# A new first stage for fused gated attention and SwiGLU: gate scratch in a tile of its own, queries and keys of batch 0 split at token 256, values cast by the transfer, weights in thirds

## The chip, the core and the metric

One core of one Trainium2 chip. The metric is device microseconds (us) of one execution of the program; lower is better.

## What is computed

```python
scores = q @ k.T / sqrt(D)                    # B, H, S, D = 8, 8, 576, 64, float32
cum    = cumsum(log(clip(f, 1e-4, 1)))        # one forget gate per token and head
scores = where(j > i, -1e9, scores + cum[i] - cum[j])
attn   = softmax(scores)
x      = (attn @ v) -> tokens x (heads*D)     # 4608 x 512
out    = (silu(x @ w_gate) * (x @ w_val)) @ w_out   # 512 -> 1536 -> 512
```

## The kernel before, in words

**The work.** Attention runs head by head, in pairs of heads (`p`, four pairs a batch). `score` (L481) multiplies 128-row blocks of keys by queries into PSUM, in four groups of blocks per head (`BANKS`). Group 0 needs only the first 256 queries and keys; groups 1 to 3 hold the rest of the triangle. Queries and keys lie transposed in the tile `QK` with 64 rows of data and four extra rows, in which the cumulated gates stand split into bf16 parts, so that the product adds the decay by itself: a score needs both the data rows and the four gate rows. `expo` (L489, ACT) takes exponentials, `mask` (L498, POOL) zeroes what lies above the diagonal, `weigh` (L512, PE) multiplies by the values in the tile `VB`, `invert` and `scale` (L519, L528, DVE) divide, and `flip` (L536, PE) and `put` write the result transposed to `xT`. The feed-forward part runs in tiles of tokens: `gate` (L613) twice per block of 128 of the 1536 columns (12 blocks, `fc`), `tanh` (ACT, L617), `silu` and `times` (DVE, L621, L624) into buffers `hh`, and `project` (L628). Batch 0's tokens are two tiles, 256 and 320 tokens, taken together block by block (`ffn(0..)`, `ffn(1..)`); after these come tiles of 512.

**The first stage.** `f` is loaded on ACT's queue (L296) into a piece of the big tile `xT`. DVE clips (L326), ACT takes logarithms (L328), DVE sums (L329) and splits the sum into parts (L331, L334, L336, L337; ACT L332). Four row transfers on ACT's queue (`row`, L341) carry the four parts for batches 0 and 1, all 576 tokens, into `QK`; `dec_out` (L351, SP) sends the parts of the other batches to memory. Queries and keys of batches 0 and 1 are loaded on SP's queue a pair of heads at a time (`ld_qk`, L364) into pieces of `xT` or of the still empty weight tile `wo`, cast to bf16 (L284), turned on PE (`turn`, L374) and copied into `QK` (`straighten`). Values are loaded in float32 on SP's queue (`ld_v`, L400) and cast by POOL, DVE or ACT. The weights `wg`, `wv`, `wo` come in quarters on POOL's queue, cast by the transfer (`weights`, L606, L609). While PE has nothing to do, up to plan time 22, it gets multiplications of no use (`dummy`, L719).

**What sets the order.** The whole order is made at build time: a small list scheduler (`Plan`) simulates the engines and queues with booked costs, gives each engine the ready operation of lowest `key`, honours `ready` times (`W_AT`, `WO_AT`, `Q1_AT`, `V1_AT`, and `release`, which admits the pairs of batches 2 to 7 at `PACE0 + n*PACE`), and hands out buffers. What it writes is one fixed instruction list per engine; on the chip each engine goes through its list in order and stops at what is not ready. Transfers of each kind (SP and ACT together, POOL alone) signal on eight semaphores in turn, so the ninth transfer waits for the first to land; the planner counts this for SP and ACT, not for POOL.

From batch 2 on, queries and keys go through memory in bf16 (`narrow`, L382, POOL's queue) and come back by transposing transfers on SP's queue (L391), with the gate rows from memory (L394).

Of the kernel before, what the change touches and what calls it, by code (L numbers as in the profile page):

```python
# [32 lines left out]
class Plan:  # L33
# [9 lines left out]
    def op(self, eng, fn, after=(), take=(), use=(), key=0.0, ready=0.0, dma=None):  # L43
        o = Op(eng, fn, list(after), list(take), list(use), key, ready, dma)
        for b in o.use:
            b.left += 1
        self.ops.append(o)
        return o
# [17 lines left out]
    def run(self, idle=None):  # L66
# [21 lines left out]
        while left:  # L88
# [4 lines left out]
            while events and events[0][0] <= t + 1e-9:  # L93
                _, _, kind, o = heapq.heappop(events)
                if kind in ("queue", "dma"):
                    busy_rings = [r for r in rings.values() if r]
                    for r in busy_rings:
                        r[0][0] -= (t - moved) / len(busy_rings)
                        while r and r[0][0] < 1e-6:
                            over, n = r.pop(0)  # L100
                            if r:
                                r[0][0] += over
                            n.done = t + 1.0
                            push(n.done, "end", n)
                            push(n.done, "done", (n, None, False))
# [4 lines left out]
                    if busy_rings:  # L110
                        push(t + min(r[0][0] for r in busy_rings) * len(busy_rings), "dma", None)
# [63 lines left out]
HALF = 256  # L175
# [11 lines left out]
PACE, PACE0 = 8.8, 70.0  # L187
# [3 lines left out]
def kernel(ctx, tc, q, k, v, f, w_gate, w_val, w_out, out):  # L191
# [16 lines left out]
    NCH = 4  # L208
# [22 lines left out]
    BF = [sb(f"BF{i}", [P, QT, 2, D], BF16) for i in range(4)]  # L231
# [3 lines left out]
    HH = [sb(f"hh{i}", [P, S], BF16) for i in range(NHH)]  # L235
# [6 lines left out]
    def ps(b):  # L242
        return bank[bank_of[b.pool] + b.i]

    early = [xT[:BH, r, S : 3 * S].bitcast(F32) for r in range(KD)]
    lf, zero, cum, r1 = early
    dec = xT[:BH, :, 3 * S : 5 * S].rearrange("p r (w s) -> p r w s", w=2)
    nat = {"nat": [xT[:QP, r, N_TOK - 2 * QT * D * 2 :].bitcast(F32).rearrange("p (h x) -> p h x", h=2) for r in range(KD)],
           "natw": [wo[:QP, KF // 4 * r : KF // 4 * (r + 1)].rearrange("p a b -> p (a b)").bitcast(F32)
                    .rearrange("p (h x) -> p h x", h=2) for r in range(4)]}  # L250
# [3 lines left out]
        {"f": 4, "s": 2, "o": 1, "t": 1, "qk": NQK, "pt0": NPT0, "pt": NPT, "vb": NVB, "nv": NNV, "nat": KD, "natw": 4, "bf": 4,  # L254
# [13 lines left out]
    def act(n):  # L268
        return 0.06 + n / 1200 + 0.06
# [31 lines left out]
    o_bf = [op(("DVE", 0.3), lambda e, i: nc.vector.memset(BF[i][QP:], 0.0), i, key=-8) for i in range(4)]  # L301

    def blank(e, what):
# [12 lines left out]
        else:  # L316
# [3 lines left out]
    o_dec = [op(("DVE", 0.3), blank, "dec", key=-7), op(("DVE", 0.9), blank, "dec1", key=-7)]  # L320
    o_qkz = op(("POOL", 0.8), blank, "qk", key=15)
    o_vb = [op(("POOL", 0.8), blank, i, key=20 + 2000 * i) for i in range(NVB)]
    o_pt = op(("POOL", 2.5), blank, "pt", key=40)
    o_edge = op(("SP", SPi), blank, "edge", after=[o_qkz], key=900, dma=0.2, ready=20)

    o_clip = op(("DVE", dve(S, False)), lambda e: nc.vector.tensor_scalar(  # L326
        out=lf, in0=lf, scalar1=1e-4, scalar2=1.0, op0=ALU.max, op1=ALU.min), after=[o_f], key=-9)
    o_ln = op(("ACT", 0.6), lambda e: nc.scalar.activation(lf, lf, AF.Ln), after=[o_clip], key=-9)  # L328
    o_scan = op(("DVE", 1.4), lambda e: nc.vector.tensor_tensor_scan(  # L329
        out=cum, data0=lf, data1=zero, initial=0.0, op0=ALU.add, op1=ALU.add), after=[o_ln, o_zero], key=-9)  # L330
    o_hi = op(("DVE", 0.7), lambda e: nc.vector.tensor_scalar_mul(dec[:, 1, 1], cum, -8.0), after=[o_scan], key=-9)  # L331
    o_up = op(("ACT", 0.6), lambda e: nc.scalar.activation(dec[:, 0, 0], cum, AF.Copy, scale=8.0),  # L332
              after=[o_scan], key=-9)
    o_r1 = op(("DVE", 0.7), lambda e: nc.vector.scalar_tensor_tensor(  # L334
        out=r1, in0=cum, scalar=-8.0, in1=dec[:, 1, 1], op0=ALU.mult, op1=ALU.subtract), after=[o_hi], key=-9)
    o_mid = op(("DVE", 0.4), lambda e: nc.vector.tensor_copy(dec[:, 2, 1], r1), after=[o_r1], key=-9)  # L336
    o_lo = op(("DVE", 0.7), lambda e: nc.vector.tensor_sub(dec[:, 3, 1], r1, dec[:, 2, 1]), after=[o_mid], key=-9)  # L337
    o_warm = op(("ACT", 1.4), lambda e: nc.scalar.activation(warm, cum[:1, :1], AF.Exp), after=[o_up], key=-9)

    def row(e, r):  # L340
        nc.scalar.dma_start(  # L341
            out=QK[D + r : D + r + 1, : FIRST * FB, :, :S].rearrange("o b (j w) s -> o (b j) w s", w=2),
            in_=dec[: FIRST * H, r].rearrange("h w s -> h (w s)"),
        )

    o_row = []
    for r, a in ((0, [o_up, o_dec[0]]), (1, [o_hi, o_dec[1]]), (2, [o_mid, o_dec[1]]), (3, [o_lo, o_dec[1]])):
        o_row.append(op(("ACT", 0.5), row, r, after=a, key=-9, dma=0.15))
# [6 lines left out]
    o_decd = op(("SP", SPi), dec_out, after=[o_up, o_lo, o_dec[0], o_dec[1]], key=60, dma=2.0)  # L355

# [6 lines left out]
    def ld_qk(e, p, nm, b):  # L363
        nc.sync.dma_start(out=nat[b.pool][b.i], in_=srcs[nm][2 * p : 2 * p + 2].rearrange("h (p t) d -> p h (t d)", t=QT))  # L364

    def cast_qk(e, bn, bb):
        dst, src = BF[bb.i][:QP].rearrange("p t h d -> p h t d"), nat[bn.pool][bn.i].rearrange("p h (t d) -> p h t d", d=D)
        copy(e, dst, src)

    def turn(e, bb, bt):  # L370
        src = BF[bb.i].rearrange("p t h d -> p t (h d)")
        t = ps(bt).bitcast(BF16)
        for n in range(QT):
            nc.tensor.transpose(t[:, n * QP : n * QP + P], src[:, n], ident)  # L374

    def straighten(e, p, x, a, bt):
        dst = QK[:D, hqk[p].i, 2 * a + x, :S].rearrange("p (c n) -> p c n", n=QT)
        src = ps(bt).bitcast(BF16)[a * D : (a + 1) * D, :S].rearrange("p (n c) -> p c n", n=QT)
        copy(e, dst, src)
# [28 lines left out]

    def values(b, n, key, after=(), ready=0.0):
        bv = Buf("nv")  # L410
        o = op(("SP", SPi), ld_v, b, n, bv, take=[bv], key=key, dma=1.53 if n < NB - 1 else 0.77, after=after,
               ready=ready)
        eng = copier(H * D, False) if b < 2 else ("POOL", pool(H * D))
# [11 lines left out]

    def queries(p, key, after=(), ready=0.0):
        done = []
        b = p // FB
        if b < FIRST:
            rest = []  # L430
            for x, nm in enumerate("qk"):
                bn, bb, bt = Buf("natw" if p in (2, 3) else "nat"), Buf("bf"), Buf("t", ("f", 30.0), ("s", 22.0))
                kk = key + 2 * x
                o1 = op(("SP", SPi), ld_qk, p, nm, bn, take=[bn], key=kk, dma=0.96, after=after, ready=ready + 0.9 * x,
                        tag=("ldqk", p))
                o2 = op({"POOL": 0.85, "DVE": 0.87} if p else ({"POOL": 0.85} if x else {"DVE": 0.87}), cast_qk, bn, bb,
                        after=[o1] + o_bf, take=[bb], use=[bn], key=kk, tag=("cast", p))
                if p in (2, 3):
                    wo_free.append(o2)
                o3 = op(("PE", mm(*[P] * QT)), turn, bb, bt, after=[o2, o_id], take=[bt], use=[bb], key=kk,  # L440
                        tag=("turn", p))
                for a in range(2):
                    first = not rest and not a
                    rest.append(op(
                        {"ACT": 0.65, "DVE": 0.75}, straighten, p, x, a, bt,
# [20 lines left out]
        else:  # L466
            done = done + o_row
        for j in range(2):
            q_ready[2 * p + j] = done
# [75 lines left out]
    def attention(p, key, parts):  # L545
# [3 lines left out]
        for n, (bks, qb, nq) in enumerate(parts):  # L549
# [5 lines left out]
            for j in range(2):  # L555
# [4 lines left out]
                for m, i in enumerate(bks):  # L560
# [5 lines left out]
                    a = op(("PE", mm(*cols)), score, h, i, bs, after=q_ready[h] + ([o_qkz] if i == 2 else []), take=[bs], use=[hqk[p]],  # L566
# [5 lines left out]
                    a = op(("POOL", 0.33), mask, h, i, after=[a], use=[hp], key=kk, tag=("mask", h, i))  # L572
# [26 lines left out]
            x_ready[p, qb] = op({"DVE": dve(m)} if not ahead else copier(m), put, p, bt, qb, nq, after=[a, ] + early_done,  # L599
# [23 lines left out]
    def times(e, n, bf, bt, bh, lo):  # L623
        nc.vector.tensor_mul(HH[bh.i][:, lo : lo + n], TH[bt.i][:, :n], ps(bf)[:, :n])  # L624

# [14 lines left out]
    def ffn(t, t0, n, hs, lo, share):  # L640
# [4 lines left out]
        for fc in range(KF):  # L645
# [14 lines left out]
            m = op(("DVE", dve(n)), times, n, bv, bt, hs[fc], lo, after=[a, b, hs[fc].first],  # L660
# [20 lines left out]
    early_done = [o_warm, o_lo, o_decd] + o_row  # L681

    LV = {0: (4, 5), 1: (14, 15)}
    queries(0, 0)
    values(0, 0, 4)
    queries(1, 5)
    values(0, 1, 9)
    queries(2, 10)
    queries(3, 20)
    for n in range(2, NB):  # L690
        values(0, n, 30 + n)
    for c in range(NCH):
        for nm, t, src in (("g", wg, w_gate), ("v", wv, w_val)):
            w_ready[nm, c] = op(("POOL", SW), weights, t, src, c, key=-3, dma=2.6, ready=W_AT[c] + (nm == "v"))
    for c in range(NCH):
        w_ready["o", c] = op(("POOL", SW), weights, wo, w_out, c, after=wo_free, key=-3, dma=2.6, ready=WO_AT[c])
# [28 lines left out]
W_AT = [15.0, 19.0, 36.0, 42.0]  # L725
WO_AT = [46.0, 48.5, 51.0, 54.0]
Q1_AT = [22.0, 24.0, 26.0, 28.0]
V1_AT = 29.0
# [31 lines left out]
```

## Time and profile before

| what | us |
|---|---|
| three runs | 419.9, 427.46, 420.07 |
| their median | 420.07 |
| span of the profiled execution (first to last instruction) | 424.4 |
| the only listed time above that span, taken as the profiled execution's own | 427.46, so 3.06 around the span |
| PE busy in the span | 388.1 (91%) |
| PE busy from 36.0 to 424.4 | 374.9 of 388.4 |
| first score on PE | 35.92 |
| last score-weighting and flip of batch 0 | before 58.2 |
| mean granted PE clock | 0.971 |

Times in the profile count from the span's start. In the strips of part 2 of the profile each digit is the busy share of one of 40 slices of 10.6 us, in tenths. A row of the chain gives a start, a length and what took it. In a table of stages, each row gives the busy time and the number of instructions of each engine, then the granted clock, the share of the DMA engines and GB/s. DMA figures count bytes written; a casting transfer from float32 to bf16 reads twice what it writes. Queue q0 is POOL's (software), q1 SP's, q10 ACT's.

### The profile page before, as it was taken

The page shows a single profiled execution, that of the slowest core. Times are in us where ns is not written, and L with a number is a line of the kernel's source. Part 1 is how long each engine was busy: PE and PEld are TensorE (multiplying, and loading weights), DVE is VectorE, ACT ScalarE, POOL GpSimd, SP SyncE. Part 2 cuts the span into 40 slices and gives each one's busy share as a digit, 9 for nine tenths or more (in the row PEclk, how much of TensorE's full clock was granted, in tenths as well). Part 3 has the DMA queues.
Part 4 walks back from the last instruction along what each step waited for, and adds up shares of the span by engine and source line. Part 5 has one row for each costly group of instructions (what it writes and reads, how often), then busy time and mean ns, then how long its engine had stood idle before and what let it go on. Part 6 is the DMA issues. An engine that isn't in the chain of part 4 may idle for free.

```text
span 424.4 us, 8314 instructions
## 1 busy us (share of the span) xinstructions
PE 388.1 (91%) x3071; PEld 227.5 (54%) x3114; DVE 230.3 (54%) x438; ACT 215.1 (51%) x442; POOL 126.9 (30%) x351
## 2 busy tenths in 40 slices
PE   3626999989999869999999999999999999999996
PEld 2514777864465535565455556555666444444542
DVE  3941688760773237742774386337643771770850
ACT  1525898622474743666366447556667431332321
POOL 5805577520152433243234314522333000000000
PEclk9965899999999999999999999999999999999999
DMA  9994799966693798569959959975401002001002
GB/s 200 185 184 57 146 214 206 214 119 170 141 145 82 177 109 162 113 106 203 190 104 209 173 126 170 165 178 102 90 27 51 25 2 75 25 2 74 26 1 86
DMA packets 111832, 51.27 MB, mean 121 GB/s; under 512 B 97328, under 2 KB 106544, under 8 KB 111408
## 3 DMA queue, kind: packets, MB, share of 16 engines
q1 hardware_dynamic: 105120, 38.65, 44.8%
q0 software_dynamic: 6400, 11.80, 16.9%
q8 instruction: 24, 0.39, 0.4%
q10 hardware_dynamic: 272, 0.30, 0.3%
q14 instruction: 16, 0.13, 0.1%
HBM read 38.34 MB, written 16.96 MB: 130 GB/s over the span
## 4 chain that ended last, share of the span: by engine, by line
PE 84%; DMA 7%; DVE 3%; ACT 3%; issue 1%; SPq 0%; ACTq 0%; POOL 0%; DVEq 0%; POOLq 0%
PE ps L613 42%; PE ps L628 22%; PE ps L481 10%; PE ps L512 7%; DMA QK<-xT 4%; DMA natv<-in_v_dram 2%; PE ps L536 2%; DMA xT<-in_q_dram 1%; ACT PT L489 1%; ACT QK L282 1%; DVE QK L284 1%; DVE xT L329 0%; ACT th L617 0%; PE ps L374 0%; DVE xT L307 0%
## 5 line engine op out<-in xcount | busy, mean ns | idle before, releaser
L613 PE MATMUL ps<-xT,wv 128*128 128x512 bf16 (+3 forms) x466 | 112.7, 359 | 0.7
L613 PE MATMUL ps<-xT,wg 128*128 128x512 bf16 (+3 forms) x471 | 111.5, 357 | 0.5
L621 DVE SCALAR_TENSOR_TENSOR th<-th,ps 128x512 f32<-128x512 f32 (+3 forms) x120 | 75.5, 629 | 64.2 <-ACT th L617 64.1
L617 ACT ACTIVATE th<-ps 128x512 f32<-128x512 f32 (+3 forms) x120 | 66.5, 555 | 83.0 <-PE ps L613 79.8
L489 ACT ACTIVATE PT<-ps 128x512 bf16<-128x512 f32 (+2 forms) x192 | 92.5, 510 | 28.2 <-PE ps L481 20.9
L628 PE MATMUL ps<-wo,hh 128*128 128x512 bf16 (+1 forms) x424 | 103.5, 379 | 1.0
L481 PE MATMUL ps<-QK 68*128 68x320 bf16 (+4 forms) x448 | 76.9, 271 | 7.1 <-DMA QK<-xT 5.3
L624 DVE TENSOR_TENSOR hh<-th,ps 128x512 bf16<-128x512 f32 (+3 forms) x120 | 75.9, 634 | 12.8 <-PE ps L613 0.8
L498 POOL TENSOR_SCALAR_AFFINE_SELECT PT<-PT 128x128 bf16<-128x128 bf16 (+1 forms) x192 | 52.7, 277 | 76.2 <-ACT PT L489 70.7
L613 PEld LDWEIGHTS <-wg 128*128 128x128 bf16 x480 | 45.3, 97 | 39.0 <-issue 0.7
L613 PEld LDWEIGHTS <-wv 128*128 128x128 bf16 x480 | 45.4, 98 | 37.0 <-issue 0.5
L628 PEld LDWEIGHTS <-hh 128*128 128x128 bf16 (+1 forms) x444 | 42.0, 98 | 39.9 <-issue 0.8
L498 POOL TENSOR_SCALAR_AFFINE_SELECT PTa<-PTa 128x256 bf16<-128x256 bf16 x64 | 25.8, 406 | 105.5 <-ACT PTa L489 104.4
L519 DVE RECIPROCAL rc<-ps 128x5 f32<-128x5 f32 (+2 forms) x64 | 12.3, 193 | 71.2 <-PE ps L512 71.0
L512 PE MATMUL ps<-VB,PT 128*128 128x65 bf16 x768 | 47.3, 195 | 3.7 <-POOL PT L498 3.7
L512 PEld LDWEIGHTS <-PT 128*128 128x128 bf16 x768 | 39.4, 99 | 19.1 <-POOL PT L498 4.8
L481 PEld LDWEIGHTS <-QK 68*128 68x128 bf16 x448 | 36.1, 101 | 20.2 <-issue 8.3
L632 ACT ACTIVATE ot<-ps 128x512 f32<-128x512 f32 (+1 forms) x37 | 22.1, 597 | 47.1 <-PE ps L628 46.4
L489 ACT ACTIVATE PTa<-ps 128x384 bf16<-128x384 f32 x64 | 30.7, 492 | 24.6 <-PE ps L481 24.4
L526 DVE TENSOR_TENSOR xn<-ps,rc 128x320 bf16<-128x320 f32 x56 | 27.5, 491 | 1.8
L284 POOL CAST VB<-natv 128x512 bf16<-128x512 f32 (+1 forms) x32 | 19.3, 617 | 16.5 <-DMA natv<-in_v_dram 13.3
L284 DVE COPY xT<-ps 128x576 bf16<-128x576 bf16 (+1 forms) x30 | 13.2, 441 | 14.3 <-PE ps L536 12.9
(48 smaller groups left out, 174.8 us busy)
## 6 DMA issues: line engine op xcount, KB each, us to landing
out_dram<-ot SPq DMA_DIRECT2D x35, 256.0 KB
natv<-in_v_dram SPq DMA_DIRECT2D x32, 256.0 KB
qk_d<-in_q_dram POOLq DMA_DIRECT2D x6, 576.0 KB, 6.9
qk_d<-in_k_dram POOLq DMA_DIRECT2D x6, 576.0 KB, 8.7
xT<-in_q_dram SPq DMA_DIRECT2D x6, 288.0 KB
xT<-in_k_dram SPq DMA_DIRECT2D x6, 288.0 KB
wg<-in_moe_w_gate_dram POOLq DMA_DIRECT2D x4, 384.0 KB, 7.8
wv<-in_moe_w_val_dram POOLq DMA_DIRECT2D x4, 384.0 KB, 9.1
```

What stands on the lines that cost most here:

```text
L284: E[e].tensor_copy(dst, src)
L481: nc.tensor.matmul(s[:, c : c + w], QK[:KR, hqk[p].i, 2 * j + 1, kt * P : (kt + 1) * P], QK[:KR, hqk[p].i, 2 * j, q0 : q0 + w], start=True ...
L489: nc.scalar.activation(place(h, i)[:, OFFS[i] : OFFS[i] + c], ps(bs)[:, :c], AF.Exp, scale=0.125)
L498: nc.gpsimd.affine_select(out=d, in_=d, pattern=pat, compare_op=ALU.is_ge, fill=0.0, base=0, channel_multiplier=-1,)
L512: nc.tensor.matmul(o[:, lo : lo + D + 1], pt[:, c : c + P], VB[hvb[b].i][:, kt, hb, : D + 1], start=first and n == 0, stop=last and n == l ...
L526: nc.vector.tensor_mul(XN[bx.i][:, qb : qb + nq, j], o, r)
L613: nc.tensor.matmul(ps(bf)[:, :n], w[:, ko, fc * P : (fc + 1) * P], xT[:, ko, t0 : t0 + n], start=(ko == 0), stop=(ko == KD - 1))
L617: nc.scalar.activation(TH[bt.i][:, :n], ps(bf)[:, :n], AF.Tanh, scale=0.5)
L621: nc.vector.scalar_tensor_tensor(out=t, in0=t, scalar=1.0, in1=ps(bf)[:, :n], op0=ALU.add, op1=ALU.mult)
L624: nc.vector.tensor_mul(HH[bh.i][:, lo : lo + n], TH[bt.i][:, :n], ps(bf)[:, :n])
L628: nc.tensor.matmul(ps(bf)[:m, :DM], HH[hs[fc].i][:, lo : lo + m], wo[:, fc, :], start=(fc == 0), stop=(fc == KF - 1))
L632: nc.scalar.activation(OT[bo.i][:m], ps(bf)[:m, :DM], AF.Copy, scale=0.5)
```

## The change

The gate scratch moves out of `xT` into the tile `hh` (one tile of 16 buffers now), which nothing else uses early. The gate arithmetic runs in two parts, tokens 0 to 255 and 256 to 575. The four row transfers become twelve, all on SP's queue: four for batch 0's first part, four for its second, four for batch 1. Queries and keys of batch 0 are loaded for four heads at a time, first tokens 0 to 255 of all heads (`ld_a`, 512-byte pieces), then, behind the first four row transfers on the same queue, the rest (`ld_b`, 1 KB pieces). Group 0 of scores waits for the first part only. Values of batches 0 and 1 are loaded by casting transfers on POOL's queue straight into `VB`. Weights come in thirds, six transfers of `wg` and `wv` and three of `wo`, put into POOL's list early. The four memsets of `BF` move from DVE to POOL. `PACE0` goes from 70.0 to 50.3 and `PACE` from 8.8 to 8.92.

In the instruction lists of the two programs this gives, in the changed one: SP: four `ld_a`, four rows, four `ld_b`, four rows, four rows, `dec_out`, then batch 1's loads. POOL: memsets of `VB`, values 0 and 1, first thirds of `wg` and `wv`, other memsets, values 2 to 4, group-0 masks of heads 0 to 5, one value block of batch 1, masks of heads 6 and 7, then **seven weight transfers in a row**, then the other masks of heads 0 to 4 and the first of head 5, then the other four value blocks of batch 1, of which the last waits on the semaphore of the third `wg` transfer; then the rest of the masks; then `narrow` for batch 2, which waits on the last `wv` third, and behind it the cast of a block of batch 1's keys. ACT: the load of the logarithm table now stands behind the wait for `f`.

```diff
-PACE, PACE0 = 8.8, 70.0
+PACE, PACE0 = 8.92, 50.3
...
-    NCH = 4
+    NCH = 3
...
-    early = [xT[:BH, r, S : 3 * S].bitcast(F32) for r in range(KD)]
-    lf, zero, cum, r1 = early
-    dec = xT[:BH, :, 3 * S : 5 * S].rearrange("p r (w s) -> p r w s", w=2)
+    lf, zero, cum, r1 = [HHA[:BH, 2 * i : 2 * i + 2].rearrange("p a s -> p (a s)").bitcast(F32) for i in range(4)]
+    dec = HHA[:BH, 8:16].rearrange("p (r w) s -> p r w s", w=2)
...
-    o_bf = [op(("DVE", 0.3), lambda e, i: nc.vector.memset(BF[i][QP:], 0.0), i, key=-8) for i in range(4)]
+    o_bf = [op(("POOL", 0.25), lambda e, i: nc.gpsimd.memset(BF[i][QP:, 4 * P : 6 * P], 0.0), i, key=0) for i in range(4)]
...
+    for k0, a, z in ((-9, 0, HALF), (5, HALF, S)):
+        n = z - a
+        c = op(("DVE", dve(n, False)), clip, a, z, after=[o_f], key=k0, tag="clip")
+        c = op(("ACT", act(n)), ln, a, z, after=[c], key=k0, tag="ln")
+        c = op(("DVE", 0.1 + n / 480), scan, a, z, after=[c, o_zero] + prior, key=k0, tag="scan")
...
+        o_row.append([op(("SP", SPi), row, r, 0, a, z, after=w, key=k0 if k0 > 0 else -4.5, dma=0.05 + n / 640, pkt=40.0, tag=("row", r))
+                      for r, w in four])
...
+    o_row1 = [op(("SP", SPi), row, r, 1, 0, S, after=gates + o_dec, key=95, dma=0.9, pkt=60.0, tag=("row1", r)) for r in range(4)]
...
+    def ld_a(e, g, nm, b):
+        E[e].dma_start(out=nat["nata"][b.i], in_=srcs[nm][4 * g : 4 * g + 4, :HALF].rearrange("h (p t) d -> p h (t d)", t=TA))
+
+    def ld_b(e, g, nm, b):
+        E[e].dma_start(out=nat[b.pool][b.i][:PB], in_=srcs[nm][4 * g : 4 * g + 4, HALF:].rearrange("h (p t) d -> p h (t d)", t=TB))
...
+    def ld_vc(e, b, n):
+        m = min(P, S - n * P)
+        nc.gpsimd.dma_start(out=VB[hvb[b].i][:m, n, :, :D], in_=v[b, :, n * P : n * P + m].rearrange("h p d -> p h d"))
...
-                    a = op(("PE", mm(*cols)), score, h, i, bs, after=q_ready[h] + ([o_qkz] if i == 2 else []), take=[bs], use=[hqk[p]],
+                    a = op(("PE", mm(*cols)), score, h, i, bs, after=q_ready[h][0] + (q_ready[h][1] if i else []) + ([o_qkz] if i == 2 else []), take=[bs], use=[hqk[p]],
...
-            w_ready[nm, c] = op(("POOL", SW), weights, t, src, c, key=-3, dma=2.6, ready=W_AT[c] + (nm == "v"))
+            w_ready[nm, c] = op(("POOL", SW), weights, t, src, c, key=-5.5 if not c else 20 + 4 * c, dma=3.0, pkt=95.0,
+                                ready=W_AT[c], tag=("w", nm, c))
...
-W_AT = [15.0, 19.0, 36.0, 42.0]
-WO_AT = [46.0, 48.5, 51.0, 54.0]
-Q1_AT = [22.0, 24.0, 26.0, 28.0]
-V1_AT = 29.0
+W_AT = [0.0, 18.9, 19.0]
+WO_AT = [18.1, 19.0, 22.1]
+Q1_AT = [29.9, 30.8, 40.4, 46.9]
+V1_AT = 0.9
```

## The prediction

> **What bounds the kernel now.** I read the strips of the page first, then the stages, then the chain of waits, and last the DMA queues in short windows. In the strips the first four slices stand out.
>
> ```profile
> PE   3626999989999869999999999999999999999996
> POOL 5805577520152433243234314522333000000000
> PEclk9965899999999999999999999999999999999999
> ```
>
> PE is poorly used up to the fourth slice and nearly full from there on, except in slices 14 and 15. The stages say it in us (PE, PEld, DVE, ACT, POOL, then clock, DMA share, GB/s).
>
> ```profile
> 20.00:30.00 10.00, 2.80 (x36) 2.31 (x34) 3.96 (x6) 1.93 (x5) 0.24 (x1) 0.72 0.98 175
> 30.00:40.00 10.00, 4.70 (x36) 3.50 (x35) 2.27 (x6) 3.91 (x10) 2.99 (x6) 0.50 0.36 62
> 60.00:144.00 84.00, 82.41 (x717) 52.05 (x723) 48.13 (x106) 45.23 (x99) 30.09 (x76) 1.00 0.83 157
> 144.00:162.00 18.00, 13.13 (x131) 8.47 (x132) 6.90 (x16) 10.60 (x24) 7.37 (x23) 0.91 0.98 131
> 162.00:420.90 258.90, 256.43 (x1859) 138.60 (x1890) 141.88 (x257) 128.27 (x256) 58.73 (x172) 1.00 0.49 100
> ```
>
> From 60 on PE is the bound (idle 1.6 and 2.5 in the two long stages, 4.9 in 144 to 162). So the change is worth what it brings forward the moment from which PE is fed. The chain over the first 44 us says what that moment waits for.
>
> ```profile
> 2.37 5.94 DMA xT<-in_q_dram
> ...
> 8.79 1.50 DVE xT L307
> ...
> 11.66 1.98 DVE xT L329
> ...
> 16.68 1.26 DVE xT L337
> ...
> 18.71 7.50 DMA QK<-xT
> ...
> 27.48 8.31 DMA QK<-xT
> 35.79 0.14 issue
> 35.92 2.08 PE ps L481 x12
> ```
>
> Gates wait for query loads that they do not need (one tile, L307), and gate rows then take 7.5 and 8.3 us to land. All data rows of `QK` were ready by 31.2 (last copy 30.39, 0.76).
>
> **Where I compare.** I take one state, S: batch 0's attention done, three of twelve blocks of the 256-token tile multiplied, five of eight blocks of batch 1's queries and keys turned. Before reaches it at 58.2 (by then 120 weighing multiplications, 24 of L613, 78 of L374, that is 48 and 30). After reaches its like when PE stands before the turn of batch 1's fourth block: it is then two blocks of L613 ahead (2 x 0.87), and two turns (0.7) and two flips (0.66) behind, 0.4 in all, which I leave out. The gain is 58.2 less that moment.
>
> **The gates.** f's 80 packets on q10 all lie in the window 2.9 to 4.3, so f lands at 4.2. DVE's two memsets (0.54, 1.50) are over by 3.0, since BF's (1.60) go to POOL. New is ACT's table load behind f: 4.2 + 1.28 = 5.5. Then ln, scan and four splits of 256 of 576 columns, the rows 0.68, 1.98, 0.91, 1.05, 0.99 and 1.26 times 0.444: 3.05, and 0.05 for each of six hand-overs: 8.9, where before stood at 17.94. The second part (3.8 by 320/576) and two copies and a cast (0.75 + 0.5 + 0.4) follow on DVE to 14.3.
>
> **The first rows.** Four issues of 0.6 on SP, the last at 9.0 to 9.6. To landing the trace shows 7.5 and 8.3 for such rows beside busy queues, and 3.4 for f (0.81 to 4.2) on an empty one. POOL's queue is filling from 4.6, so I take 6: first score at 15 (12.4 to 17.3), against 35.92.
>
> **The second part.** The four `ld_b` stand behind these rows on SP: issue 9.6 to 11.7. In the window 24 to 26 q1 moved nothing, though its loads were issued from 22.39 on: 3.6 us to the first packet at 26. So data flow from 13.2. 1.31 MB at 264 GB/s (window 10 to 13) are 5.0; at q1's share beside q0 (0.41 MB in 27 to 29) 6.4. Last landing 20 to 22, I take 21.5. Cast 1.1 (0.61 by 1024/512, less its fixed part), turn 0.85, copy 0.75: 24.2. The second rows wait for the first rows' semaphores (15 and on), are issued by 17.4 and land at 20.8 to 25.7. Two blocks of L613 stand ahead of the next scores in PE's list: 1.74, twice that at half clock. Groups 1 to 3 start at 27, against 40.1.
>
> **ACT's share.** Eight heads of 0.59 + 0.49 + 0.44 are 12.2: exponentials end at 39.2 at the earliest, with two tanh of 0.37 near 40. By ACT alone, S would be at 41.5.
>
> **POOL's list and its queue.** Here the change adds waits. Behind the seven weight issues (0.76 each, 5.3) stand the masks of groups 1 to 3; POOL reaches them near 27, in time. But the last value block of batch 1 waits for the third `wg` transfer, the remaining masks of heads 5 to 7 stand behind it, PE's weighing behind these; and `narrow` waits for the third `wv`, with a cast of keys behind it, for which PE's list waits too. q0 must have moved by then: 5632 value packets (4608 and 1024) and six thirds of 512. Prices:
>
> ```profile
> q1 hardware_dynamic: 2556, 0.66, 133.6%
> ...
> q0 software_dynamic: 543, 0.40, 131.2%
> ...
> q0 software_dynamic: 1419, 1.37, 90.4%
> ...
> q0 software_dynamic: 352, 0.27, 109.9%
> ```
>
> These are the windows 14 to 17 (256-byte packets, q1), 42 to 44 and 24 to 26 (768 bytes written, q0) and 69 to 78 (mostly 1 KB written, q0). A third costs 512 / 158 = 3.25. A value packet (256 read, 128 written) is not shown on q0. Low end: as on q1, 852 a us, 6.6 us in all. High end: as 768-byte packets on q0, 272 a us, 20.7. The two sizes on q0 took 77 and 92 ns; the line through them gives 39 ns at 128 bytes, 530 a us, 10.6 us, which I take as nearest to a small packet on that queue. So q0 needs 10.6 + 16.3 = 26.9 up to the third `wg`, 30.1 up to the third `wv`. q1 moves beside it about 17 us of its own (`ld_b` 5.0, decay 1.7, four loads of batch 1 4.5, three value blocks 3.6, the tail of `ld_a` 2). Both at once carry 333 GB/s (0.71 MB and twice 0.31 in 26 to 30) against 264, a factor of 1.26. From q0's first packets at 4.6 (issue 2.6, and 2 as for L609): third `wg` at 4.6 + 43/1.26 = 39, third `wv` at 42. Then one issue (1.0), eight masks (2.2): 42.2; last weighing, reciprocal, scaling and the scores ahead in PE's list, about 3: 45. By the other way: 42 + 0.53 + 0.85 for issue and cast, 43.4. I take S at 46.5, 1.5 for hand-overs and a cold clock (0.50 in the trace from 26 to 44.8).
>
> [...]
>
> **The rest.** After S the same work stands on the same bound engine. Removed casts of values (0.4 to 0.8 on DVE, ACT, POOL) are off PE's path; `project` in three groups has the same twelve multiplications; the release times, 50.3 + 23 x 8.92 = 255.5 for the last pair against 272.4, only order the plan. I add 0 for the new plan, between -4.9 and +4.9: the idle time of 144 to 162, which comes from one value load that met two `narrow` transfers (10.07 us in the chain) and may be gone or come back elsewhere.
>
> **The sum.** 58.2 - 46.5 = 11.7. The profiled execution (424.4 and 3.06 around it, 427.46) would become 415.8. Its 7.4 above the median I put down to that stall and the slow clock after it (4.9 and 1.7), so from the median: 420.07 - 11.7 = 408.4.
>
> **Rivals.** First, ACT is the only limit: q0 moves values as q1 does (6.6), the third `wv` lands by 39 and the masks keep up, S at 41.5, time 403.4. For it: 264 packets a us on q0 alone; against it: POOL's list. Second, hidden anyway: value packets at the high end, 10.1 us more on q0 with nothing of it shared, S at 56.6, time 418.5: the first scores come 20 us sooner and the masks wait. Third, slower: q0 runs as in 24 to 26, 176 packets a us whatever their size; values cost 32 in place of 10.6, POOL sits at the third `wg` until 60, S at 67.9, time 429.8. It makes the kernel slower by over 2% from S at 66.6 on, that is below 183 value packets a us. For it speaks that this window is q0's own start; against it, that it ran half again as fast at 42 to 44. Fourth, the rows still hold everything: they land 8.3 after issue and the second ones after them at 27; scores start at 29 and S moves by no more than 2, 410.
>
> **How the numbers follow.** The forecast with the fourth rival beside it 0.5 (own range 404 to 413), ACT alone 0.15, hidden 0.25, slower 0.1. About 2% (8.4 us) is what a measurement of this kernel tells from no change. Faster, under 411.7: 0.15 and most of 0.5, with a little of the third case's near side: 0.62. Same: 0.28, slower: 0.1. The range goes from 400 (ACT alone and 3 of the later stall) to 420 (the high end for values and nothing else won).
>
> **What would show it.** Right: clip near 4.3, the last first-part row issued near 9, first score at 12 to 17, groups 1 to 3 near 27, then POOL idle before its last value issue until the third `wg` lands near 39, the weighing of head 5 behind it, and S near 46. Wrong: q0's value packets near 77 ns or more; masks that wait for the seven weight issues well beyond 27; first rows later than 18; or a stall after S that before does not have.

## The result: slower by a tenth, and the profile after

The changed kernel takes 462.0 us (median of four runs, 460.65 to 463.76); the kernel before took 421.95 in the same comparison (419.9 to 427.46, four runs). The ratio is 1.097, 95% interval 1.091 to 1.103. The forecast was 408.4, in 400 to 420. Ratios here and below are over undisturbed runs alone; medians and spreads are over all runs, which differ by up to 4% within one kernel. The profiled execution has a span of 458.9 and took 460.65, so some 1.8 lie around the span, not the 3.06 that the forecast took; 427.46 was hardly the profiled execution of before.

The strips of the changed kernel answer to those of before: there PE was poorly used in four slices and nearly full from then on, here it has holes up to slice 14, and the clock drops to 0.5 in slice 6 and to 0.6 to 0.8 in several others.

```profile
PE   5769379777999389999979999799999999999996
ACT  3858666774357247764755565356662332332331
PEclk9978759898999869999997999989999999999999
```

The same stages in us (PE, PEld, DVE, ACT, POOL, then clock, DMA share, GB/s):

```profile
20.00:30.00 10.00, 6.00 (x58) 4.52 (x56) 7.20 (x14) 6.39 (x8) 7.96 (x14) 0.73 1.38 120
30.00:40.00 10.00, 7.97 (x64) 5.26 (x62) 5.11 (x7) 7.16 (x16) 3.09 (x12) 0.84 1.15 257
60.00:144.00 84.00, 74.06 (x598) 46.27 (x597) 48.47 (x93) 49.27 (x85) 21.09 (x57) 0.91 0.52 99
144.00:162.00 18.00, 9.08 (x90) 5.43 (x88) 5.21 (x12) 6.60 (x14) 4.25 (x13) 0.88 1.05 112
162.00:455.00 293.00, 284.83 (x2081) 153.60 (x2081) 149.09 (x276) 141.28 (x283) 65.61 (x194) 0.97 0.49 95
```

In 20 to 40 PE does 14.0 us of work where before did 7.5: the early start is there. But in 60 to 144 it idles 9.9 us (before 1.6) and runs at 0.91, and in 144 to 162 it idles 8.9 (that stall is another matter, told under "The later stall"). The chain of waits of the changed kernel names what it stands on:

```profile
10.88 5.21 DMA QK<-hh
16.14 2.74 PE ps L581 x16
...
19.45 1.60 ACT QK L296
21.07 1.58 DVE QK L298
...
30.81 1.60 ACT QK L296
32.44 1.58 DVE QK L298
...
46.64 2.09 ACT QK L296
48.74 2.09 ACT QK L296
...
53.59 2.08 DVE QK L298
...
56.54 2.09 ACT QK L296
58.66 2.10 DVE QK L298
...
61.63 2.09 ACT QK L296
63.75 2.08 DVE QK L298
```

Rows land at 16.1 and scores start at once, as forecast. What comes then is no transfer and no mask: it is the copy of turned queries and keys out of PSUM into `QK` (`straighten`), 1.6 us for batch 0's second part and 2.09 for batch 1, the two of a turn one after the other. In the whole chain these copies take 8.5% of 458.9, 39 us; in the chain of before they take 1.2%, 5 us. The groups by form show its price in the changed kernel (busy, mean ns of one, idle before):

```profile
L296 ACT ACTIVATE QK<-ps 64x576 bf16<-64x576 bf16 x11 | 23.0, 2086 | 6.5 <-PE ps L419 5.6 <-PE ps L612 0.6
L298 DVE COPY QK<-ps 64x576 bf16<-64x576 bf16 x5 | 10.4, 2074 | 12.5 <-ACT QK L296 12.5
L298 DVE COPY QK<-ps 64x640 bf16<-64x640 bf16 x5 | 7.9, 1579 | 4.5 <-ACT QK L296 4.1 <-PE ps L419 0.3
L296 ACT ACTIVATE QK<-ps 64x512 bf16<-64x512 bf16 x5 | 3.7, 735 | 2.7 <-DVE QK L298 2.4 <-PE ps L419 0.3
```

and in the kernel before:

```profile
L284 DVE COPY QK<-ps 64x576 bf16<-64x576 bf16 x17 | 12.7, 753 | 9.1 <-ACT QK L282 7.9 <-PE ps L374 1.1
L282 ACT ACTIVATE QK<-ps 64x576 bf16<-64x576 bf16 x15 | 9.6, 646 | 11.4 <-issue 8.1 <-DVE QK L284 2.1 <-PE ps L374 1.1
```

Same shape, same bytes, 2.8 to 3.2 times the time. The halves of a turn follow one another in both kernels (7.9 and 12.5 us in these rows), so a turn costs 1.4 us before and 4.2 after. The reason is in the code: the cast no longer puts two heads side by side, so the turned halves hold even and odd tokens, and each copy writes every other token. Its innermost loop reads neighbouring columns of the turned block, so successive 2-byte values land 8 bytes apart (`straighten_b`) or 12 (`straighten`), and 4 in `straighten_a`, which took 0.74 for 512 columns.

### The profile page after: what moved, and what is told of

The parts are those of the page before. It is cut to its first block, busy times and chain, and to the rows that moved or that the text cites. A ratio compares the mean times of both kernels' runs of the same rounds, so it can differ in the third digit from the quotient of the medians.

```text
span 458.9 us, 8374 instructions
## 1 busy us (share of the span) xinstructions
PE 407.6 (89%) x3121; PEld 234.5 (51%) x3121; DVE 237.9 (52%) x438; ACT 237.8 (52%) x445; POOL 125.6 (27%) x353
## 4 chain that ended last, share of the span: by engine, by line
PE 74%; DMA 7%; ACT 7%; DVE 5%; SPq 4%; issue 1%; POOL 0%; ACTq 0%; DVEq 0%
PE ps L713 35%; PE ps L729 20%; PE ps L581 9%; PE ps L612 6%; ACT QK L296 5%; DVE QK L298 3%; DMA natv<-in_v_dram 3%; SPq L452 3%; DMA QK<-dec_d 2%; PE ps L636 2%; PE ps L419 1%; DMA QK<-hh 1%; DMA hh<-in_f_dram 1%; ACT PT L589 1%; SPq L461 1%
## 5 line engine op out<-in xcount | busy, mean ns | idle before, releaser
L713 PE MATMUL ps<-xT,wv 128*128 128x512 bf16 (+3 forms) x480 | 117.0, 368 | 1.6 <-DVE QK L298 1.6
L713 PE MATMUL ps<-xT,wg 128*128 128x512 bf16 (+3 forms) x480 | 116.9, 367 | 0.0
L729 PE MATMUL ps<-wo,hh 128*128 128x512 bf16 (+1 forms) x444 | 108.3, 385 | 0.0
L581 PE MATMUL ps<-QK 68*128 68x320 bf16 (+4 forms) x448 | 78.4, 277 | 17.0 <-DMA QK<-dec_d 13.2
L725 DVE TENSOR_TENSOR hh<-th,ps 128x512 bf16<-128x512 f32 (+3 forms) x120 | 76.1, 634 | 15.0 <-PE ps L713 3.8
L713 PEld LDWEIGHTS <-wv 128*128 128x128 bf16 x480 | 47.2, 100 | 41.2 <-issue 2.9
L713 PEld LDWEIGHTS <-wg 128*128 128x128 bf16 x480 | 47.0, 101 | 40.5 <-issue 1.7
L581 PEld LDWEIGHTS <-QK 68*128 68x128 bf16 x448 | 38.2, 103 | 35.3 <-DMA QK<-dec_d 9.9
L612 PE MATMUL ps<-VB,PT 128*128 128x65 bf16 x768 | 45.5, 198 | 3.6 <-POOL PT L598 3.6
L733 ACT ACTIVATE ot<-ps 128x512 f32<-128x512 f32 (+1 forms) x37 | 22.1, 597 | 49.4 <-PE ps L729 48.3
L296 ACT ACTIVATE QK<-ps 64x576 bf16<-64x576 bf16 (+2 forms) x19 | 31.4, 1652 | 12.4 <-PE ps L419 9.1
L298 DVE COPY QK<-ps 64x640 bf16<-64x640 bf16 (+2 forms) x13 | 20.4, 1570 | 17.4 <-ACT QK L296 16.6
```

The lines of the kernel that those rows point to most:

```text
L296: nc.scalar.activation(dst, src, AF.Copy)
L298: E[e].tensor_copy(dst, src)
L581: nc.tensor.matmul(s[:, c : c + w], QK[:KR, hqk[p].i, 2 * j + 1, kt * P : (kt + 1) * P], QK[:KR, hqk[p].i, 2 * j, q0 : q0 + w], start=True ...
L612: nc.tensor.matmul(o[:, lo : lo + D + 1], pt[:, c : c + P], VB[hvb[b].i][:, kt, hb, : D + 1], start=first and n == 0, stop=last and n == l ...
L713: nc.tensor.matmul(ps(bf)[:, :n], w[:, ko, fc * P : (fc + 1) * P], xT[:, ko, t0 : t0 + n], start=(ko == 0), stop=(ko == KD - 1))
L729: nc.tensor.matmul(ps(bf)[:m, :DM], HH[hs[fc].i][:, lo : lo + m], wo[:, fc, :], start=(fc == 0), stop=(fc == KF - 1))
```

## The experiments

To compare first stages I sum useful work: every multiplication in the trace but the dummies counts its columns / 2400 + 0.0025 us (in the trace of before, at a clock of 1.00, fours of 512 columns start every 0.864 us from 202.56 to 210.34, and four of 65 take 0.12 from 219.50), each kind scaled to its full number, since a few records are missing (before has 466 of the 480 with `wv`). The state S of the forecast (58.2 before) is 18.0 us of such work.

| us at work of | 18 (S) | 40 | 85 | 115 | 355 | ratio to before |
|---|---|---|---|---|---|---|
| before | 58.2 | 80.4 | 126.7 | 164.9 | 406.5 | 1 |
| changed | 61.0 | 90.8 | 145.8 | 188.4 | 440.7 | 1.097 (1.091 to 1.103) |
| e4_order_b1 | 54.2 | 76.1 | 124.2 | 166.5 | 418.8 | 1.028 (1.021 to 1.034) |
| e1_order | 51.0 | 72.9 | 120.0 | 160.0 | 402.6 | 1.004 (0.998 to 1.010) |
| e11_order_pace | 48.1 | 71.2 | 119.5 | 152.2 | 392.9 | 0.977 (0.970 to 0.984) |
| e7_scratch | 51.5 | 73.7 | 120.0 | 154.2 | 396.3 | 0.986 (0.980 to 0.991) |

**The copies.** Theory A: they are the loss. B: POOL's waits and queue. C: the new plan.

e1_order, the same addresses in ascending order, successive values 4 bytes apart (in `straighten_b` alike):

```diff
-dst = QK[:D, hqk[p].i, x::2, :S].rearrange("p j (c u t) -> p j u c t", u=QT // 2, t=2)[:, :, :, :, u]
-src = ps(bt).bitcast(BF16)[u * D : (u + 1) * D, :S].rearrange("p (j u c) -> p j u c", j=2, u=QT // 2)
+dst = QK[:D, hqk[p].i, x::2, :S].rearrange("p j (c u t) -> p j c u t", u=QT // 2, t=2)[:, :, :, :, u]
+src = ps(bt).bitcast(BF16)[u * D : (u + 1) * D, :S].rearrange("p (j u c) -> p j c u", j=2, u=QT // 2)
```

> The copies of turned queries and keys out of PSUM write the same addresses, but walk over tokens in ascending order (steps of 4 bytes) instead of jumping 8 or 12 bytes. Theory A (the loss is the price of these copies, 1.6 us at 8 bytes and 2.09 at 12, two one after the other per turn): they fall to about 0.7 to 0.85 us, like the 0.72 of the first part, groups 1 to 3 start near 28 instead of 36, and the time is 405 to 418. Theory B (POOL's waits and the transfers hold the first stage): the copies may get shorter, the time stays above 440. Theory C (the new plan has stalls of its own after 100 us, 158.5 to 162.8 the longest): half of the loss stays, 425 to 440.

e4_order_b1, the same in `straighten` (batch 1) alone:

> Only the 16 copies of batch 1 go in ascending order; the eight of batch 0's second part keep their 1.6 us. Theory A, with its two parts adding up: groups 1 to 3 stay near 36 as in the changed kernel, 8 to 9 us behind the run in which both are reordered, so the time is 6 to 10 us above that run, 412 to 427. Theory B: above 440 as the others. Theory C: 430 to 445.

e2_head, the cast interleaves heads as before, each copy writes whole heads without gaps:

```diff
-copy(e, BF[bb.i][:m, :n], src().rearrange("p h x -> p (h x)"))
+s = src().rearrange("p h (t d) -> p h t d", d=D)
+copy(e, BF[bb.i][:m, :n].rearrange("p (t h d) -> p h t d", h=s.shape[1], d=D), s)
...
-dst = QK[:D, hqk[p].i, x::2, :S].rearrange("p j (c u t) -> p j u c t", u=QT // 2, t=2)[:, :, :, :, u]
+dst = QK[:D, hqk[p].i, 2 * u + x, :S].rearrange("p (c t) -> p c t", t=QT)
...
```

> The layout of before is put back in the cast (two heads side by side in each 128 columns), so that each copy out of PSUM writes whole heads without gaps; everything else of the change stays. Theory A: copies 0.64 (ACT) and 0.76 (DVE) for 576 columns as in the kernel before, casts a little dearer (0.75 to 0.9 instead of 0.4 to 0.8), time 403 to 415, within 1% of the run with ascending order. Theory B: above 440. Theory C: 425 to 440.

e3_slowcopy, the reverse: the kernel before with only that cast and those copies of the changed one:

> The kernel before with only the cast without interleaving and the copies out of PSUM in steps of 12 bytes of the changed kernel; all else as before. Theory A: all 32 copies take about 2.09 us, batch 0's data rows are ready 15 to 20 us after 31, and the time goes up by 20 to 45 us, to 440 to 465. Theory B and C: 420 to 428.

Measured: e1 427.47 (ratio in the table), e4 437.71, e2 430.59 (1.010, 1.002 to 1.018), e3 445.98 (1.047, 1.040 to 1.055). The copies of e1, then of e2:

```profile
L296 ACT ACTIVATE QK<-ps 64x576 bf16<-64x576 bf16 x11 | 8.9, 813 | 3.4 <-PE ps L419 2.5 <-PE ps L612 0.7
L298 DVE COPY QK<-ps 64x640 bf16<-64x640 bf16 x5 | 4.4, 873 | 4.0 <-ACT QK L296 3.7 <-PE ps L419 0.3
```

```profile
L296 ACT ACTIVATE QK<-ps 64x576 bf16<-64x576 bf16 x11 | 7.1, 644 | 3.7 <-PE ps L420 3.0 <-PE ps L613 0.7
```

Theory A holds for what it names and B falls: the order of the loops alone brings 9.3% (1.097 to 1.004, 39 us of 421.95). In the traces of the changed kernel, e1, e2 and e4 the instructions of VectorE, ScalarE, GpSimd and SyncE are the same and stand in the same order, so no other order of work can be behind it. How the 39 us divide is less sure: by the ratios 29 in batch 1 (1.097 to 1.028) and 10 in batch 0, by the traces at work 355 about 22 and 16. Put alone into the kernel before, with the cast that belongs to them, the slow copies cost 4.7%. But no run came to 403 to 418: against the forecast's ratio of 0.972 about 3% was still missing, and e1 and e2 ended in the range that C gave.

**The later stall.** At work 40 to 85, e1 is 7 us ahead of before; at 100 it is 3 behind (144.7 against 141.7). Its stages show where:

```profile
120.00:144.00 24.00, 17.06 (x156) 10.41 (x155) 5.85 (x14) 9.69 (x20) 6.07 (x19) 0.86 0.90 142
```

PE idles 6.9, waiting for gate rows (6.7 us) that stand behind transposes on SP's queue, and then runs at a clock of 0.56 to 0.59 from 132 to 140. Before has its like at 144 to 162, where the chain waits for a value load on SP's queue, and the changed kernel at 145 to 163. In each, two transfers of POOL (`narrow`, 18 KB packets) go through at that moment.

e11_order_pace, e1 with the release times of before:

```diff
-PACE, PACE0 = 8.92, 50.3
+PACE, PACE0 = 8.8, 70.0
```

> The changed kernel with the copies in ascending order, and the release times of before (70 and 8.8 instead of 50.3 and 8.92), nothing else. Theory C (the early release puts the transfers to memory and SP's transposes against each other, which gave the stall at 119 to 135): the stall shrinks below 4 us and the 7.4 us of the first stage show, 415 to 420. Rival (the stall comes from the order of SP's list whatever the release): stays within 424 to 430.

e14_before_pace, the reverse edit on the kernel before:

> The kernel before with the release times of the changed one (50.3 and 8.92 instead of 70 and 8.8) and nothing else. Theory C (admitting the later batches sooner puts their transfers, and the work that they feed, against the first stage and each other, whatever the first stage is): slower by 1 to 3%, 426 to 436. Rival (only in the changed plan did these numbers fall on a bad order): within 1%.

e15_order_mid, e1 with 60.0 and 8.86:

> The changed kernel with the copies in ascending order and release times between the two (60.0 and 8.86). Theory C as a matter of degree: between 414 and 424, about 417 to 421. Rival (each number gives another order, good or bad by chance): outside of these two, or at one end of them.

e16_head_pace, e2 with the old release times:

> The changed kernel with copies that write whole heads (0.64 and 0.76 us instead of 0.81 in ascending order) and the old release times. Theory C: it gains as much by the release times as the ascending order did (2.7%), 412 to 419 instead of 430.6. Rival: its stalls come from elsewhere, 424 or more.

Measured: e11 420.14 in the median, but its four times lie in two groups, 413.1 and 414.1, 426.2 and 427.1; the ratio of 0.977 is that of the first two, the medians over all runs (420.14 to 422.78) give 0.994. e14 434.18, 1.018 (1.011 to 1.024); e15 429.82, 1.011 (1.007 to 1.016); e16 419.36 in the median against e2's 430.59, its best run 410.9. The stage of e11 in which e1 stalled:

```profile
120.00:144.00 24.00, 24.00 (x227) 14.46 (x226) 9.74 (x21) 15.78 (x35) 8.77 (x27) 1.00 0.57 137
```

The early release costs 1.8% on before, 2.7% on e1 by the ratios (1.3% by the medians) and 2.7% on e2 by the medians. It is not a matter of degree: the times between (1.011) are no better than the early ones (1.004, the intervals overlap). They give another order: at over 90 of its 217 places SP's list in e15 holds another instruction than in e1, and so does e11's; in e15 PE waits 8.1 us for gate rows between 200 and 240. That the early release costs is clear on before; on e1 it hangs on the faster two of e11's times; by which rule it costs is not shown.

**The transfers to memory.** e5_before_fine and e6_order_fine cut `narrow` into 2 KB packets, on before and on e1:

```diff
-out=qk_dram[2 * b + x, :HSD].rearrange("(a c) -> a c", c=512),
+out=qk_dram[2 * b + x, :HSD].rearrange("(y a c) -> a y c", y=2, c=1024),
```

> The kernel before, in which the transfers that write bf16 queries and keys to memory go in pieces of 2 KB instead of 18 KB (1024 elements, alternating between the two halves of the tensor). Theory D (behind these transfers the small packets of SP's queue wait, because each large packet keeps an engine for 1.4 us and more; that makes the stall in 144 to 162): the transposes behind the third such pair stay under 2 us each instead of 15.3 for four, PE's idle time in that stage falls from 4.9 to under 2, the time by 3 to 9 us. Theory E (it is the bytes, however they are cut): stall and time stay within 1%.

> The changed kernel with the copies in ascending order, and the transfers to memory in pieces of 2 KB. Theory D: the stall at 119 to 135 (PE idle 6.9 in 120 to 144) goes, and what the first stage gains (7.4 us at a like amount of work) reaches the end: 412 to 420, 1.5% or more below the kernel before. Theory E: 424 to 429, as with the order alone.

Measured: e5 421.39, 0.995 (0.990 to 1.000); e6 424.37, 0.999 (0.994 to 1.005). The transposes that met these transfers, before and then in e5:

```profile
146.48 15.34 SPq L391 DMA_TRANSPOSE QK<-qk_d  x4
```

```profile
143.94 9.79 SPq L391 DMA_TRANSPOSE QK<-qk_d  x4
```

Each theory holds in part. The stall shrinks (PE idle in 144 to 162 from 4.9 to 0.6), the time by 0.5%; in e6 the stall only gets shorter (work 85 to 100 takes 21.8 us instead of 24.7) and another one comes at 160 to 175 (22.8 instead of 15.6). In before, while 18 KB packets of 1.4 us and more passed (148 to 161), SP's queue moved 1 to 119 of its 256-byte packets a us in 149 to 159, against 480 to 1000 in 147, 148 and 161 to 163. But with 2 KB packets it still moved only 8 to 134 a us in 147 to 155, so the size of the packets is not the whole cause; what differs is that the two transfers were through in 10 us instead of 13. How the DMA engines share their time between the queues is not shown.

e13_order_pace_fine, e11 with these packets:

> The changed kernel with the copies in ascending order, the old release times, and the transfers to memory in pieces of 2 KB. If the pieces help wherever a transfer to memory meets SP's queue, it gains another 0.5%, 409 to 412 where the run without them took 413.1 and 414.1; if what is left of the stalls is not theirs, 412 to 416.

417.75 in the median (412.3 to 419.0), 0.978 (0.971 to 0.984): no further gain. e8_order_lead admitted `narrow` 8 us sooner in e1:

> The changed kernel with the copies in ascending order, and the transfers to memory admitted 8 us sooner by the planner (release less 20 instead of less 12), in their large pieces. If the stall at 119 to 135 is a matter of too short a lead, it shrinks and the time falls by 3 to 7 us, to 418 to 424; if the large packets hold SP's queue whenever they come, the stall moves with them and the time stays at 424 to 430.

434.59, but this kernel computes wrong values, so nothing is rested on its time.

**The gate scratch alone.** e7_scratch is the kernel before with only `lf`, `zero`, `cum`, `r1` and `dec` moved to `hh` (made one tile, whose later products wait until the gate work is done); up to the first scores its lists hold the same work in the same order.

```diff
-early = [xT[:BH, r, S : 3 * S].bitcast(F32) for r in range(KD)]
-lf, zero, cum, r1 = early
-dec = xT[:BH, :, 3 * S : 5 * S].rearrange("p r (w s) -> p r w s", w=2)
+lf, zero, cum, r1 = [HHA[:BH, 2 * i : 2 * i + 2].rearrange("p a s -> p (a s)").bitcast(F32) for i in range(4)]
+dec = HHA[:BH, 8:16].rearrange("p (r w) s -> p r w s", w=2)
...
```

> The kernel before with only the gate scratch moved out of the big tile; queue, rows and order of the lists as before. By the prediction's account the memset of 1.50 us no longer waits until 8.8, but on VectorE the cast of the first queries now stands ahead of the sum and waits for its load, so the gates end near 15 to 16 instead of 17.9, the rows land 2 to 3 us sooner, and the time falls by 0 to 4 us. The rival (the memset's wait was the whole delay): gates end near 11, first score at 30 or before, time 5 to 6 lower.

417.72, ratio 0.986 (0.980 to 0.991), some 6 us: past the first expectation and near the rival, so the wait of the memset was most of the delay of the gates. Its chain:

```profile
11.89 0.75 DVE hh L337
...
14.74 4.78 DMA dec_d<-hh
19.54 9.10 DMA QK<-hh
28.64 0.14 issue
28.77 2.08 PE ps L481 x12
```

The memset now starts at 3.55 instead of 8.79, the gates end at 12.64 instead of 17.94, the first score comes at 28.8 instead of 35.9, and 6.7 of these 7.1 us are left at work 40. In this chain the last row waits for the transfer of the other batches' parts. e10_scratch_rows puts that transfer behind the rows; e9_scratch_fine is e7 with 2 KB packets, e12_scratch_rows_fine has all three:

```diff
-o_decd = op(("SP", SPi), dec_out, after=[o_up, o_lo, o_dec[0], o_dec[1]], key=60, dma=2.0)
+o_decd = op(("SP", SPi), dec_out, after=[o_up, o_lo, o_dec[0], o_dec[1]] + o_row, key=60, dma=2.0)
```

> The kernel before with the scratch moved, and the gate parts of the other batches sent to memory behind the four gate rows, not ahead of the last of them. In the run with the scratch alone that row was issued at 19.5, behind this transfer, and landed at 28.6. Theory A (the last row sets the first score): it is issued by 15 to 16.5, lands by 25, first score 3 to 5 us sooner, time 2 to 5 us lower, 413 to 416. Rival: the rows land late whenever they are issued (queues full), 416 to 419.

> The kernel before with the scratch moved (417.7) and the transfers to memory in pieces of 2 KB (alone 0.995 of before). If both gains are of different places they add up: ratio 0.975 to 0.985, 413 to 416. If the pieces only move a stall along the plan, it stays at 417 to 420.

> All three together on the kernel before: scratch moved, the other batches' gate parts behind the rows, pieces of 2 KB. If they add up, 409 to 414, ratio 0.965 to 0.98; if later stalls take it back, 414 to 419.

Measured: e10 419.95, 0.989 (0.983 to 0.995), first score at 28.3: the last row was issued no sooner (19.7). In ACT's list it stood behind an issue that waited until the first row had landed (at 17.9) and behind a copy, so the edit did not do what it was for. e9 415.79, 0.983 (0.978 to 0.987), the best median of all runs; e12 419.93, 0.990 (0.985 to 0.995).

## Why the prediction was wrong, step by step

- **The gates and first rows** were right to within 2 us: f landed at 4.8 (4.2), the last early row was issued near 10.9 (9.0) and landed 5.2 later at 16.1 (15).
- **POOL's list and q0**, from which the forecast took S at 46.5, were priced nearly right but held nothing up: batch 0's 128-byte value packets took 32 ns (the line gave 39), up to 1203 a us. In the changed kernel and in e11 POOL waits for no weight transfer before 60. In e1 it does, 0.45 and 2.05 us, with the third `wv` landed at 45.2 (42 forecast), but PE waits for no mask between 31 and 52. Neither the limit of 46.5 nor the slower rival came from here. The weight issues took 0.75 to 0.80 us each (0.76 forecast, 0.91 the longest in before). POOL's two waits in e1; the columns end with the idle time before and its releaser:

```profile
45.19 0.54 POOL L443 DMA_DIRECT2D qk_d<-in_q_dram  x1 [0.45 <-DMA wv<-in_moe_w_val_dram]
...
48.62 0.51 POOL L443 DMA_DIRECT2D qk_d<-in_k_dram  x1 [2.05 <-DMA wo<-in_moe_w_out_dram]
```

- **The step that failed** is "Cast 1.1, turn 0.85, copy 0.75: 24.2", and with it the eight turns of batch 1, which were not priced at all. The copy's price was taken from a row of the same shape but another access pattern. It was 1.6, twice per turn, in four turns, and 2.09 in batch 1. What went before was priced well: the last `ld_b` packet landed at 22.5 (21.5 forecast), the second rows at 22.1 (20.8 to 25.7). But groups 1 to 3 started at 34.5, not 27: 12.0 us after that landing, where the forecast left 5.5. The order of these copies alone is worth 39 us of the time (e1). Even with the copies in order it is 7.8 us, from 24.1 to 31.9: the forecast took one cast, one turn and one copy, where four turns, each with two copies one after the other, follow on one another, three of their four casts (1.0 us each) on ACT beside the copies.
- **"I add 0 for the new plan"**, between -4.9 and +4.9, measured about +11 by the ratios of e1 and e11 (1.004 against 0.977; 5.5 by their medians, each over that of before) and +7 on the kernel before (e14): the release times do not "only order the plan". Its own sign of being wrong, "a stall after S that before does not have", is the one at 145 to 163.
- **The sum that was left** came out near, in part by luck: with these two taken out (e11), S comes at 48.1 (46.5 forecast), 10.1 sooner than before (11.7), and the ratio is 0.977 (0.972 forecast) over the faster two runs, 0.994 by the medians. But in e11 POOL issues `narrow` only at 64.6, and q0 does not set S; groups 1 to 3 start at 29.2 (27), and what follows goes by exponentials, turns and copies. Near values by another path do not confirm the path.
- **Rivals**: all four looked at queues, lists and exponentials. The rival that would have caught it (an edited copy that writes with gaps) was visible in the diff's new `rearrange` and was not among them.
- **What is open**: which order of transfers makes the early and the middle release times slow, and why e11's times lie in two groups. Early values and weights were not undone singly; all of the change but its scratch, copies and release times is worth what lies between e7 (0.986) and e11 (0.977), whose intervals overlap, so a gain is not shown.

## What to carry to other kernels

When a diff changes a `rearrange`, write down for each operand how many bytes lie between successive elements of the innermost loop, and price the instruction anew even if shape and engine stay (here 0.65 us without gaps and 2.09 at 12 bytes, for 576 columns on ACT). Try the smallest part of a change by itself: moving a scratch tile off a falsely shared one gave 1.4%, where the whole rebuilt first stage gave 2.3% at best (e11). And constants that tune a fixed plan are part of a change: test them apart.

## What the hardware showed unexpectedly

Copies of 2-byte values from PSUM to SBUF on 64 partitions, ACT and DVE alike: without gaps 0.64 (ACT, e2) and 0.75 (DVE, before) for 576 columns; 4 bytes apart, in e1, 0.81 (576) and 0.87 to 0.88 (640); 8 apart, in the changed kernel, 1.58 to 1.59 (640), 2.5 ns a value; 12 apart 2.07 to 2.09 (576), 3.6 ns a value. The slow forms read PSUM in order, while the quick ones of 576 and 640 columns jump 192 or 160 bytes there at nearly every value, so the price of the slow ones lies in the writes; `straighten_a` also reads in order, writes 4 bytes apart and took 0.74 and 0.72 for 512. Nor does jumping in PSUM look free on DVE: its copies that read in order and write without gaps (`xT<-ps`, 128 partitions) took 0.45 for 576. Steps of 8 bytes took 1.8 times as long as steps of 4 (1.58 against 0.87 on DVE, 1.59 against 0.88 on ACT, 640 columns), and these 1.26 times as long as none on ACT (0.81 against 0.64) and 1.06 times on DVE (0.81 against 0.76 in e2). So for these writes no step that was run is free; by which rule the price grows with the step is not shown.
